# Filter inputs first, all sine tables at the beginning, weight conversions in two parts, and loads one step ahead, in a convolution and expert kernel

## The chip, the core and the metric

The kernel runs on one core of one Trainium2 chip. The metric is device time in microseconds (us), the median of several executions. Besides whole times, I quote the lengths of stages, read from one profiled execution of each kernel; the start of a stage is the start of its first matmul on TensorE.

## The reference

The first half is a long convolution by Fourier transforms, with a filter made by a two-layer network. The second half is an expert layer that multiplies its hidden values by their cosine.

```python
# x, v: (4, 12480, 128) float32; pos_emb: (12480, 64)
h_filt = (np.maximum(pos_emb @ w1, 0.0) @ w2) * np.exp(-0.01 * pos)[:, None]
u = x * v
Uf = np.fft.rfft(u, n=L, axis=1)            # L = 2 * 12480
Hf = np.fft.rfft(h_filt, n=L, axis=0)
y = np.fft.irfft(Uf * Hf[None], n=L, axis=1)[:, :12480, :]
z = (x * y).reshape(49920, 128)
h = z @ w_in                                # w_in (128, 2048), float64
out = (h * np.cos(h)) @ w_out               # w_out (2048, 128), float64
```

## The kernel before

A transform is two stages of matmuls, f1 and f2, with a twiddle between them; the inverse is i1 and i2. The sine tables are made on the chip. The float64 weights come as pairs of 32-bit words and are converted to float32 in eight pieces each. One batch is transformed at the start; the other three are interleaved with the expert matmuls through generators, whose yields say how many expert matmul steps pass before the next piece.

```python
def to_float32(pool, dst, raw):                      # one piece of a weight
    power = pool.tile([P, WCOL], U32, name="power")
    nc.vector.tensor_scalar(out=power, in0=hi, ...)           # exponent bits
    nc.gpsimd.tensor_scalar(out=power, in0=power, ...)        # twice
    nc.vector.tensor_scalar(out=sig, in0=hi, ...)
    nc.scalar.activation(high, sig, ...); nc.scalar.activation(low, lo, ...)
    nc.gpsimd.tensor_tensor(high, high, low, op=ALU.add)
    nc.vector.scalar_tensor_tensor(out=power, in0=hi, in1=power, ...)  # waits for GpSimd
    there = low if dst.space == DRAM else dst
    nc.gpsimd.tensor_tensor(there, high, power, op=ALU.mult)
    # ... store of there, if dst is in DRAM

# f1: one of two engines takes the whole eviction of matmul pair b
def f1_takers(b):
    if b % 2 == 0:
        return nc.scalar.copy, ...
    return nc.vector.tensor_copy, ...

def units(n, steps, before, mm, after, parts, ahead=2):
    for j in range(min(ahead, n)):
        before(j)                                    # loads
    # ... matmuls and evictions of n steps, with yields
    yield REST

REST = 1.5
U_STEPS, F1_STEPS, F2_STEPS, I1_STEPS, I2_STEPS = 2.0, 0.8, 3.3, 0.8, 1.5

def u_units(b, bufs, u, engine, side="left"):        # u = x * v, sums, differences
    # ... units(...) with u_multiply(tiles[j], half, engine), u_sums(...)
    clear_gap(u)                                     # a memset on GpSimd

# the start
for i in range(NCH):                                 # 11 chunks of filter rows
    if i + 3 < NCH:
        pes[i + 3] = filter_load(pool, i + 3)        # pe: 4 buffers
    if i + 1 < NCH:
        peTs[i + 1] = filter_turn(pool, bank, pes.pop(i + 1), ident)
    filter_hidden(pool, bank, aT, i, peTs.pop(i), w1_sb, windows[i])
    for _ in range(2):
        next(first_u)                                # x, v loads, products on GpSimd
    if i == 0:
        forward_tables(pool)                         # 6 sine tables on VectorE
# ... filter output beside u; f1 of the filter beside the rest of u
with tc.tile_pool(name="tables", bufs=1) as pool:    # in f1 of u
    inverse_tables(pool)                             # 10 sine tables on GpSimd
with tc.tile_pool(name="convert", bufs=1) as pool:   # w_in, beside the rest of f1
    convert = convert_units(pool, [(wind[:, c], w) for c, w in in_pieces])
    # ... one step of convert every 6 units
# ... f2; i1 beside the conversion of w_out; i2 and experts
```

## Time and profile before

The median was 3912.47 us (3909.58 to 3913.06, three runs). The stages below are used in the whole document.

| stage | what runs | from, us | length, us |
|---|---|---|---|
| A | filter layers, 11 chunks | 0 | 57.2 |
| B | filter output, beside u = x v | 57.2 | 36.9 |
| C | f1 of the filter, beside the rest of u | 94.1 | 47.0 |
| D | f1 of u, tables, w_in conversion | 141.1 | 87.7 |
| E | f2 of both | 228.8 | 105.2 |
| F | i1, w_out conversion | 334.0 | 70.2 |
| G | first i2 groups, to the first expert matmul | 404.2 | 24.0 |
| H | experts, with the other three batches between | 428.2 | 3481.5 |

In the profile, PE is TensorE, DVE VectorE, ACT ScalarE, POOL GpSimd and SP the queue that issues the transfers; PEld is TensorE loading its weights. An eviction is the copy of a finished matmul result out of PSUM, TensorE's result memory, by VectorE or ScalarE; until then its place there is not free: in D of the kernel before TensorE waited 18.5 us in all for such copies by ScalarE. ScalarE's instruction ACT_TABLE_LOAD stands twice in this trace, at 0.73 and at 13.08 us, 1.28 us each; these are the loads that the prediction counts. The granted clock is the share of TensorE's full clock that the profile records, 1.00 or 0.50 at any moment of the traces of the kernel before; in a longer window it is the mean. Behind a wait for the memset (L350), from 1512 to 1519 us, it was 0.52 in the kernel before, and 1.00 from 1519 to 1524 us. A line of the view of waits reads: engine, what it wanted to write, what it waited for, then us in total, times, longest. "L395" is line 395 of that kernel; the change moved the lines, so L374 before is L395 after. The prediction shows the lines of before that carry it.

### The profile page before, as it was taken

What the parts mean: (1) busy time and instruction counts of PE and PEld (TensorE: products, weight loads), DVE (VectorE), ACT (ScalarE), POOL (GpSimd) and SP (SyncE); (2) the same over time, 40 slices, a digit from 0 to 9 for tenths busy, and PEclk for the clock granted to TensorE, in tenths of its full rate; (3) what the DMA queues carried; (4) which work ended last, traced back from release to release, by engine and by line L of the source; (5) the groups of instructions that cost most, each with busy time, mean ns of one, the idle gap of its engine ahead of it and who ended that gap; (6) DMA issues with size and microseconds to landing.
All of it is one profiled execution on the core that took longest, in us unless ns stands there. A gap on an engine that the chain in (4) does not pass through costs nothing.

```text
span 3909.7 us, 47024 instructions
## 1 busy us (share of the span) xinstructions
PE 3740.2 (96%) x13450; PEld 2126.6 (54%) x13450; DVE 2783.3 (71%) x5739; ACT 2500.7 (64%) x4639; POOL 2596.0 (66%) x2340
## 2 busy tenths in 40 slices
PE   5798798999999999999999999999999999999999
PEld 3766554655456555654466555544466644444444
DVE  3787798677776787677776886777865566666666
ACT  3554566766665456766665556766655477777777
POOL 6555587468874565588854665588844477777776
PEclk7899899999999999999999999999999999999999
DMA  4143444012210562022201660122202500000000
GB/s 131 51 119 105 139 139 121 11 55 67 75 49 9 164 175 64 23 70 69 73 23 31 174 181 26 39 68 69 70 12 80 170 24 17 20 19 17 22 17 14
DMA packets 208363, 273.90 MB, mean 70 GB/s; under 512 B 16968, under 2 KB 145768, under 8 KB 207976
## 3 DMA queue, kind: packets, MB, share of 16 engines
q1 hardware_dynamic: 208104, 270.89, 24.0%
q8 instruction: 108, 1.77, 0.2%
q14 instruction: 151, 1.24, 0.1%
HBM read 191.57 MB, written 79.26 MB: 69 GB/s over the span
## 4 chain that ended last, share of the span: by engine, by line
PE 79%; POOL 4%; DVE 4%; ACT 3%; DMA 2%; issue 1%; SPq 0%; POOLq 0%; DVEq 0%; ACTq 0%
PE ph L651 31%; PE acc L676 26%; PE cv L676 5%; PE cv L447 4%; PE cv L422 4%; PE cv L374 3%; PE cv L404 3%; POOL f L660 3%; PE ph L123 2%; DMA hd<-h 1%; ACT cs L665 1%; DVE slots L432 1%; DVE k L657 1%; DVE xt L362 1%; DVE gt L667 1%
## 5 line engine op out<-in xcount | busy, mean ns | idle before, releaser
L660 POOL TENSOR_TENSOR f<-a,k 128x512 f32<-128x512 f32 x1568 | 1984.5, 1266 | 1060.7 <-DVE k L657 1051.4
L651 PE MATMUL ph<-at,w_in_sb 128*128 128x512 f32 x3136 | 1606.1, 593 | 17.3 <-DVE gt L667 16.9
L654 ACT ACTIVATE a<-ph,quarter 128x512 f32<-128x512 f32 x1568 | 1072.5, 684 | 802.5 <-PE ph L651 793.8
L676 PE MATMUL acc<-gt,w_out_sb 128*128 128x512 f32 x2688 | 1378.2, 594 | 8.2 <-ACT ot L682 8.1
L667 DVE TENSOR_TENSOR gt<-ph,cs 128x512 f32<-128x512 f32 x1568 | 1078.0, 687 | 319.8 <-ACT cs L665 294.0
L657 DVE TENSOR_SCALAR k<-a 128x512 f32<-128x512 f32 x1568 | 787.6, 502 | 636.2 <-ACT a L654 611.7
L665 ACT ACTIVATE cs<-f 128x512 f32<-128x512 f32 x1568 | 980.2, 625 | 343.9 <-POOL f L660 342.2
L676 PEld LDWEIGHTS acc<-gt,w_out_sb 128*128 128x128 f32 x2688 | 507.5, 190 | 663.7 <-issue 624.9
L651 PEld LDWEIGHTS ph<-at,w_in_sb 128*128 128x128 f32 x3136 | 556.2, 190 | 360.9 <-issue 262.4
L417 POOL TENSOR_TENSOR slots<-slots,t 120x256 f32<-120x256 f32 x384 | 312.1, 819 | 72.3 <-PE ps L404 37.0
L447 PEld LDWEIGHTS cv<-slots,tm 96*104 96x104 f32 x1920 | 245.4, 173 | 113.2 <-issue 100.4
L447 PE MATMUL cv<-slots,tm 96*104 96x128 f32 x1920 | 257.7, 278 | 16.8 <-DMA tm<-td 13.0
L676 PE MATMUL cv<-gt,w_out_sb 128*128 128x512 f32 (+1 forms) x448 | 222.2, 578 | 1.0 <-DVE gt L667 1.0
L422 PEld LDWEIGHTS cv<-cs,slots 120*96 120x96 f32 x1536 | 175.6, 167 | 65.3 <-issue 62.2
L422 PE MATMUL cv<-cs,slots 120*96 120x120 f32 x1536 | 182.2, 266 | 1.1 <-POOL slots L417 0.8
L374 PEld LDWEIGHTS cv<-c,slots 104*124 104x124 f32 x768 | 134.7, 195 | 85.8 <-issue 59.7
L404 PE MATMUL cv<-slots,w 124*120 124x256 f32 x576 | 173.0, 380 | 0.0
L374 PE MATMUL cv<-c,slots 104*124 104x192 f32 x768 | 153.8, 330 | 19.3 <-POOL slots L350 19.3
L404 PEld LDWEIGHTS cv<-slots,w 124*120 124x120 f32 x576 | 103.3, 184 | 121.9 <-issue 113.5
L368 POOL TENSOR_TENSOR slots<-xt 104x256 f32<-104x256 f32 x120 | 120.5, 1004 | 41.7 <-PE ph L651 19.1
L676 PEld LDWEIGHTS cv<-gt,w_out_sb 128*128 128x128 f32 x448 | 84.8, 190 | 102.5 <-issue 99.5
L432 DVE TENSOR_TENSOR slots<-cv,other 96x240 f32<-96x240 f32 x384 | 133.8, 395 | 5.4 <-ACT other L430 4.4
(121 smaller groups left out, 2564.6 us busy)
## 6 DMA issues: line engine op xcount, KB each, us to landing
h<-hd SPq DMA_DIRECT2D x144, 240.0 KB
tm<-td SPq DMA_DIRECT2D x90, 312.0 KB
xt<-in_x_dram SPq DMA_DIRECT2D x120, 208.0 KB
vt<-in_v_dram SPq DMA_DIRECT2D x120, 208.0 KB
xs<-in_x_dram SPq DMA_DIRECT2D x120, 208.0 KB
zd<-zs SPq DMA_DIRECT2D x120, 208.0 KB
zb<-zd SPq DMA_DIRECT2D x97, 256.0 KB
w<-wd SPq DMA_DIRECT2D x144, 116.2 KB
```

Source lines behind the costliest of these rows:

```text
L374: nc.tensor.matmul(ps[0:KE, i * 2 * N1:(i + 1) * 2 * N1], u[:, b, 0:KE, i], c1[0:u.shape[0], :, :].rearrange("p r k -> p (r k)"), start=Tr ...
L404: nc.tensor.matmul(ps[0:N2, i * 2 * D:(i + 1) * 2 * D], w[:, i, :], src[0:KE], start=True, stop=True)
L417: nc.gpsimd.tensor_tensor(y[:, r], y[:, r], t[:, r], op=op)
L422: nc.tensor.matmul(ps[0:N1, (i * 2 + r) * N2:(i * 2 + r + 1) * N2], parts[0:N2, r, :, b, i], cs[:, r, :], start=True, stop=True)
L447: nc.tensor.matmul(ps[0:R, i * D:(i + 1) * D], t[:, i, r, :], slots[0:N1, :, place, :], start=(r == 0), stop=(r == 1))
L651: nc.tensor.matmul(ph[:, 0:m], w_in_sb[:, c * P:(c + 1) * P], ats[n][:, 0:m], start=True, stop=True)
L654: nc.scalar.activation(a[:, 0:m], ph[:, 0:m], AF.Identity, bias=quarter[:, 0:1], scale=INV_TWO_PI)
L657: nc.vector.tensor_scalar(out=k[:, 0:m], in0=a[:, 0:m], scalar1=ROUND, scalar2=ROUND, op0=ALU.add, op1=ALU.subtract)
L660: nc.gpsimd.tensor_tensor(f[:, 0:m], a[:, 0:m], k[:, 0:m], op=ALU.subtract)
L665: nc.scalar.activation(cs[:, 0:m], f[:, 0:m], AF.Sin, scale=TWO_PI)
L667: nc.vector.tensor_tensor(gt[:, 0:m], ph[:, 0:m], cs[:, 0:m], op=ALU.mult)
L676: nc.tensor.matmul(accs[n][:, 0:m], w_out_sb[:, c, :], gt[:, 0:m], start=(c == 0), stop=(c == NFC - 1))
```

## The change

The intent is to give TensorE its filter inputs at once, to move table work out of D, to take VectorE's wait for GpSimd out of the conversions, and to have data ready when a later batch changes its stage. Cut to its core:

```diff
-def to_float32(pool, dst, raw):
-    power = pool.tile([P, WCOL], U32, name="power")
+def float32_parts(pool, raw):
+    power = pool.tile([P, WCOL], U32, name="power", bufs=2)
 ...                                   # as before, to the sum of high and low
+    return power, high
+def float32_join(dst, raw, power, high):
     nc.vector.scalar_tensor_tensor(out=power, in0=raw[:, :, 1], in1=power, ...)
-    there = low if dst.space == DRAM else dst
+    there = power.bitcast(F32) if dst.space == DRAM else dst
 ...                                   # convert_units: parts of piece i, then join of i - 1
+            if i < len(pieces):
+                half = float32_parts(pool, raws[i])
+            if i > 0:
+                float32_join(pieces[i - 1][0], raws[i - 1], *last)
 ...                                   # Tables: on VectorE; a yield before each Sin
+        yield
         nc.scalar.activation(dst, t, AF.Sin, scale=TWO_PI / turn)
 ...                                   # the inverse tables are stored to DRAM, reloaded before f2
 ...                                   # units(): a yield 0.0 behind the first loads
-REST = 1.5
-U_STEPS, F1_STEPS, F2_STEPS, ... = 2.0, 0.8, 3.3, ...
+REST = 3.0
+U_STEPS, F1_STEPS, F2_STEPS, ... = 2.0, 0.8, 2.9, ...
 ...                                   # u_units
+                if j == H // UA - 2:
+                    clear_gap(u)
-            clear_gap(u)              # behind the last sum
 ...                                   # i2 beside the next batch's u
-            if i >= 4:
+            if i >= 5:
 ...                                   # forward_units: first i2 loads ahead of i1
+    next(back)
     yield from i1_units(bank)
 ...                                   # the start: all pe first, then x and v
+                for i in range(1, NCH):
+                    pes[i] = filter_load(pool, i)
+                first_u = u_units(0, 3, slots,
+                                  lambda j, half: nc.gpsimd if half == 0 or 6 <= j < 18
+                                  else nc.vector)
                 for i in range(NCH):
-                    for _ in range(2):
-                        next(first_u)
+                    for _ in range(2):
+                        next(sines, None)
+                    if i >= 5:
+                        for _ in range(3):
+                            next(first_u)
 ...                                   # expert rows are loaded later in a block
-                if c == 0 and n + 2 < NALL:
+                if c == NFC - 4 and n + 2 < NALL:
                     load(n + 2)
```

## The prediction

> **What bounds the kernel now.** I began with the page, parts 1 and 2: busy time of each engine, then the span in 40 slices of 98 us.
>
> ```profile
> PE 3740.2 (96%) x13450; PEld 2126.6 (54%) x13450; DVE 2783.3 (71%) x5739; ACT 2500.7 (64%) x4639; POOL 2596.0 (66%) x2340
> PE   5798798999999999999999999999999999999999
> PEclk7899899999999999999999999999999999999999
> ```
>
> TensorE (PE) is busy 96% of the span; its unfilled slices are the first seven. So from some 690 us on only the gaps between matmuls can be won, and the rest must come from the start. I cut the span where the matmul line changes and asked for each stage's busy times (length, then PE, PEld, DVE, ACT, POOL, granted clock, DMA share, GB/s).
>
> ```profile
> 0.00:57.20 57.20, 23.61 (x67) 12.73 (x67) 10.63 (x38) 22.68 (x41) 28.66 (x45) 0.77 0.44 105
> 57.20:94.10 36.90, 28.47 (x120) 20.63 (x121) 26.49 (x75) 11.03 (x30) 34.76 (x46) 0.87 0.57 167
> 94.10:141.10 47.00, 45.70 (x256) 43.91 (x257) 42.66 (x172) 37.35 (x188) 26.45 (x43) 0.95 0.26 75
> 141.10:228.80 87.70, 61.58 (x258) 54.30 (x256) 52.67 (x152) 43.76 (x133) 46.87 (x71) 0.77 0.12 37
> 228.80:334.00 105.20, 96.44 (x384) 67.00 (x384) 92.33 (x287) 52.89 (x139) 67.82 (x96) 0.98 0.58 167
> 334.00:404.20 70.20, 56.32 (x512) 54.57 (x512) 47.69 (x155) 28.95 (x84) 32.12 (x34) 0.98 0.15 47
> 404.20:428.20 24.00, 13.43 (x76) 12.92 (x77) 9.54 (x23) 8.30 (x22) 8.15 (x11) 0.61 0.71 213
> 428.20:690.00 261.80, 232.22 (x859) 125.76 (x858) 232.50 (x385) 162.88 (x316) 204.27 (x178) 0.98 0.45 130
> 690.00:3909.70 3219.70, 3182.43 (x10925) 1734.79 (x10923) 2268.82 (x4456) 2132.91 (x3691) 2146.93 (x1819) 0.99 0.21 61
> ```
>
> In order: A, filter layers; B, filter output; C, the filter's first transform; D, that of u (with inverse sine tables and the w_in conversion); E, second transform; F, inverse transform with the w_out conversion; G, first groups of output, until the first expert matmul at 428.2; H, the last two rows, experts with the other batches between. In B POOL is the fullest (34.8 of 36.9). D is the hole: C has as many matmuls and takes 47 us, D 87.7, with no engine full. The chain of waits, on the stages D, F and H in turn (H: PE only), names what fills the holes.
>
> ```profile
> PE ps L374 <- ACT slots L381: 18.5, 5, 15.1
> DVE power L145 <- POOL power L134: 17.2, 8, 2.2
> DVE power L130 <- DMA raw<-in_moe_w_in_dram: 15.9, 1, 15.9
> ...
> DVE power L145 <- POOL power L134: 17.2, 8, 2.2
> ...
> PE cv L374 <- POOL slots L350: 19.3, 3, 6.5
> PE ph L651 <- DVE gt L667: 16.9, 15, 2.6
> PE cv L447 <- DMA tm<-td: 13.0, 3, 5.0
> ```
>
> DVE stands 15.9 us for the raw words of w_in, because their buffers lie where the table pool was and GpSimd finishes the tables only at 164; then 8 x 2.15 us for GpSimd in the middle of each conversion, with the evictions that free PE's PSUM banks queued behind. In H, three batches each pay a memset wait (L350) and a table load wait (tm).
>
> [...]
>
> ```profile
> 1515.36 1.64 PE L374 MATMUL cv<-c,slots 104*124 104x192 f32 x4 [6.52 <-POOL slots L350]
> 1516.79 1.91 PE L651 MATMUL ph<-at,w_in_sb 128*128 128x512 f32 x2
> 1518.50 1.30 PE L676 MATMUL acc<-gt,w_out_sb 128*128 128x512 f32 x2
> 1519.63 0.81 PE L374 MATMUL cv<-c,slots 104*124 104x192 f32 x4
> ```
>
> Start to start, the first four L374 take 1.43 us against 0.65 later, L651 1.71 against 0.86, L676 1.13 against 0.86: 1.9 us lost on top of the 6.5. [...] L145's wait holds ready evictions. [...] Here the 104x256 multiply takes 0.72 us on POOL, 0.41 alone on DVE. [...] The trace shows 1.28 us, and the instruction order of the changed kernel has two loads, as before, so interleaving sines with relus adds none.
>
> **The change part by part.**
>
> A. Before, SyncE's queue stood from 7.7 to 28.3 us at a vt load with no free buffer, pe loads behind it; PE waited 14.5 us for pe and 27.3 for ACT, itself behind six sines. Now all pe go first: 11 x 240 KB at the some 200 GB/s seen in the first slices is about 14 us. The chunks then run at PE's 2.4 us (its spacing at 32 to 37 us). Tables put on DVE 16 sines at about 1.05 us, some 17 us, beside that. From chunk 5 on POOL has 1.2 + 0.73 + 0.97 = 2.9 us a chunk: chunk 5 at about 27, the last done near 43. 44 instead of 57.2: **-13**.
>
> B. u now advances 38 units (12.7 pairs) here instead of 45 (15); POOL takes 2.43 us a pair, so 31 instead of 36.5, just over PE's 28.5. 32 instead of 36.9: **-5**.
>
> C. In exchange 11.3 pairs instead of 8 to 10 fall here, with half the multiplies on DVE: 11.3 x (0.43 + 0.45) = 10 us, against 5.6 us in the 42.7 now. DVE gets to 37 + 10 = 47 us plus waits for POOL and the vt load in its queue. Estimate 54: **+7**.
>
> D. Tables gone from here (10 sines on GpSimd), raw words loaded early. DVE's own work: 32 x (0.55 + 0.36 + 0.35), start to start 1.23 us = 39.4, and 8 conversions x 0.95 = 7.6: 47 us. The join is now queued 14 units (some 5 us) behind its parts, POOL needs 3.1 us for those, so no wait. PE needs 46, ACT 33 + 7. 49 with the start of E: **-39**.
>
> E. Same pools, same hd stores; DVE at 2.02 us for each of 48 steps sets it. **-1**.
>
> F. The joins' 17.2 us on DVE go; PE becomes the bound: 512 x 0.105 = 54, and a cold start. 56: **-14**.
>
> G. The four first x and v loads now come behind zb(0), which the first transpose waited 9 us for. 21: **-3**.
>
> Start: -13 - 5 + 7 - 39 - 1 - 14 - 3 = **-68**; the first expert matmul at about 360.
>
> H. clear_gap is issued two steps early: 19.3 us of waits and 3 x 1.9 of slow clock, 25. tm and xs are asked for before i1: 13.0 and about 9 of slow clock (2.6 to 3.3 each in the timeline), 22. The forced burst of 88 L422 at 1265 goes as well, by my count of the paces (some 358 expert steps to the next batch's output, the 31st group needed at 364 instead of 352), but it was work, not idling. Against this, 428 to 690 is close to DVE's limit (232.5 of 261.8), a pace of 3.4 instead of 3.5 gives DVE less time per group, and of each wait a little may stay: I give back 5. **-42**.
>
> Sum: -110 of 3912: about 3803.
>
> **Rivals.** *C takes it back.* DVE waits in turn for POOL and for vt in C, and PE's evictions stand behind, as the conversions' did in D. For: [...] x/v came at 170 GB/s in B. Against: vt waits were on POOL, and C has DMA at 0.26. If so +10 to +20: 3815 to 3823. *Nothing in H.* The wait for the memset may be a wait for the pipe: at 682.5 it ran directly behind the expert work (f, L660), and the last sum of u would then hold f1 as long. For: POOL ran sum, f, memset back to back. Against: three REST steps of 1.7 us now lie between that sum and f1, instead of half as many. If half stays, +12 to +20. *DVE full from 428 to 690.* It is 89% busy; faster pacing could open more gt waits (16.9 us): +5 to +10. *Better still:* A's first chunks or C cost less than said, -10.
>
> **Range and chances.** Start: A to C together some +-12, D +-8, F and G +-5; H +-12. In squares about 20 us, so 8 in 10 lie within some 26: 3778 to 3830. Faster by over 2% means below 3834: 0.91. Same 0.085, slower 0.005, since no part adds PE work.
>
> **What would show it.** First expert matmul near 360; first filter-output matmul near 44; f2 beginning near 180; no DVE wait of a join for POOL in D or F; PE waits for the memset and for tm together under 8 us after 428; PE idle there 35 us or so instead of 66. Wrong would be: DVE waits for xt in C over 10 us with C beyond 60 us; the memset's wait reappearing under the name of the sum; or E longer because the reloaded tables or w stores wait for freed memory.

## The result, and the profile after

The changed kernel took 3844.14 us in the median (3840.34 to 3847.06, four runs), beside 3912.19 us for the kernel before (3909.58 to 3913.06, four runs). The ratio is 0.9827, with a 95% interval of 0.981 to 0.9844. The time fell by 1.7%, about 68 us where 110 had been predicted, and so by less than the 2% to which the prediction had given 0.91.

The page of the changed kernel, busy times and two rows of the 40 slices:

```profile
PE 3728.1 (97%) x13450; PEld 2119.9 (55%) x13450; DVE 2819.6 (73%) x5803; ACT 2494.4 (65%) x4639; POOL 2551.1 (66%) x2274
...
PE   6988889999999999999999999999999999999999
...
PEclk8899999999999999999999999999999999999999
```

TensorE's count is the same and the start is still where it isn't full. The stages again (columns as in the prediction), here A, C, D, F and G:

```profile
0.00:52.20 52.20, 26.49 (x67) 12.98 (x67) 32.88 (x87) 23.32 (x51) 23.63 (x38) 0.74 0.43 110
...
84.20:149.65 65.45, 62.05 (x256) 56.07 (x257) 53.72 (x211) 37.46 (x189) 21.24 (x28) 0.72 0.30 87
149.65:207.70 58.05, 46.62 (x259) 44.74 (x257) 48.27 (x130) 40.83 (x122) 28.56 (x32) 0.92 0.15 42
...
313.10:372.30 59.20, 55.42 (x512) 54.94 (x512) 49.50 (x155) 28.48 (x85) 30.43 (x36) 0.96 0.18 55
372.30:396.00 23.70, 10.79 (x60) 10.44 (x61) 7.04 (x16) 6.46 (x17) 5.80 (x9) 0.66 0.52 156
```

C is longer than before although it has the same number of matmuls, at a granted clock of 0.72. Against the prediction:

| stage | before | predicted | after | after less predicted |
|---|---|---|---|---|
| A | 57.2 | 44 | 52.2 | +8 |
| B | 36.9 | 32 | 32.0 | 0 |
| C | 47.0 | 54 | 65.4 | +11 |
| D | 87.7 | 49 | 58.0 | +9 |
| E | 105.2 | 104 | 105.4 | +1 |
| F | 70.2 | 56 | 59.3 | +3 |
| G | 24.0 | 21 | 23.7 | +3 |
| first expert matmul at | 428.2 | 360 | 396.0 | +36 |
| H | 3481.5 | 3439.5 | 3442.6 | +3 |

H has the predicted length. The view of TensorE's waits after 396 us begins so; neither the memset nor tm is in it any more:

```profile
PE ph L677 <- DVE gt L693: 19.6, 18, 2.3
PE acc L702 <- ACT ot L708: 5.3, 11, 1.1
PE ph L126 <- DMA zb<-zd: 4.9, 2, 3.1
```

The start did not. Three views show what stood in its place.

**A.** The timeline of VectorE in the changed kernel (start, length, both in us), then of GpSimd and of ScalarE:

```profile
18.23 0.28 DVE L210 TENSOR_SCALAR moved<-prod,quarter_p 124x120 f32<-124x120 f32 x1
18.61 1.03 DVE L213 TENSOR_SCALAR turned<-moved 124x120 f32<-124x120 f32 x1
```

```profile
18.29 1.27 POOL L338 TENSOR_TENSOR slots<-relu,window 128x480 f32<-128x480 f32 x1 [3.09 <-ACT relu L336]
```

```profile
23.70 0.28 ACT L219 ACTIVATE tw_w<-turned 124x96 f32<-124x96 f32 x1 [1.92 <-DVE turned L217]
23.89 0.54 ACT L328 COPY peT<-ps 128x480 f32<-128x480 f32 x1
```

A table instruction that takes 0.19 to 0.28 us elsewhere took 1.03 us while GpSimd multiplied by the window. From 18 to 40 us this comes once in every chunk. L213 ends at 19.64 us, just behind GpSimd's end at 19.56. The last two lines show how that reaches TensorE: the Sin waits 1.92 us for VectorE, and the copy of the next chunk's input (peT), ready since its transpose on TensorE ended at 20.36 us, stands behind it until 23.89.

**C.** Slices of 5 us of the changed kernel, columns as above:

```profile
100.00:105.00 5.00, 5.00 (x32) 5.00 (x32) 4.71 (x18) 4.56 (x24) 2.22 (x3) 1.00 0.44 129
...
110.00:115.00 5.00, 3.72 (x20) 3.13 (x21) 4.71 (x17) 2.57 (x14) 3.07 (x4) 1.00 0.52 154
...
120.00:125.00 5.00, 4.98 (x16) 3.95 (x14) 4.74 (x20) 2.38 (x12) 1.46 (x2) 0.50 0.28 85
...
135.00:140.00 5.00, 4.99 (x15) 4.48 (x16) 2.79 (x12) 1.61 (x8) 0.00 (x0) 0.50 0.00 0
```

At first 32 matmuls pass in 5 us, then 20 with VectorE full (4.71 of 5), then 15 or 16 at half clock. At 135 us VectorE has room again (busy for 2.79 of 5), but TensorE is still at half clock, though it is recorded as busy for 4.99 of 5, as for 4.98 in the slice before. The view of TensorE's waits names ScalarE's evictions there (3.2 us in C) and not VectorE's; that VectorE sets the pace is read from its busy time, and tested below. The weight loads show what goes on from 132 us:

```profile
132.04 2.41 PEld L395 LDWEIGHTS ps<-c,ftile 96*124 96x124 f32 x8 [0.52 <-ACT slots L402]
134.97 2.41 PEld L395 LDWEIGHTS ps<-c,ftile 96*124 96x124 f32 x8 [0.52 <-ACT slots L402]
137.90 2.41 PEld L395 LDWEIGHTS ps<-c,ftile 96*124 96x124 f32 x8 [0.52 <-ACT slots L402]
140.84 6.25 PEld L395 LDWEIGHTS ps<-c,ftile 96*124 96x124 f32 x20 [0.52 <-ACT slots L402]
```

Matmuls start 0.32 us apart, but after every eight TensorE waits for an eviction, and that step takes 0.54 us. From 141 us this wait is gone, and at 147.74 us the clock is full again. This slow stretch lasted 30.7 us, from 117.02 us on. Three other executions with an unchanged C (see below) were read in windows of 20 us from 100 to 160 us; the slow time there comes to some 10 us in a0 (clock 1.00, 0.77, 0.97), some 17 us in y3 (1.00, 0.64, 0.94) and some 34 us in y5 (0.87, 0.50, 0.77). The 30.7 us are nine times 3.41 us; in the traces of the kernel before and of the changed one every slow stretch, but for the one that the trace's end cuts, is a whole multiple of 3.41 us. Cut into pieces of 3.41 us, the last piece of the 30.7 us held 11 matmul starts, and no earlier piece more than 10. So in this stretch the clock came back after the piece with the most starts. (A stretch of 6.8 us from 82.88 us ended after a piece of 10, so no rule is shown.)

**D.** The view of VectorE's waits in D of the changed kernel:

```profile
DVE power L133 <- DMA wind<-power: 5.8, 6, 1.8
DVE w L277 <- DMA wind<-power: 2.1, 1, 2.1
```

The wait for GpSimd is gone, and so is that for the raw words. A new one is there: a converted piece is now built in the tile power, which has two buffers, and the piece after next waits until it is stored.

### The profile page after: what moved, and what is told of

Same layout as the page of the kernel before. It is cut to its first block, busy times and chain, and to the rows that moved or that the text cites. A ratio compares the mean times of both kernels' runs of the same rounds, so it can differ in the third digit from the quotient of the medians.

```text
span 3838.6 us, 47111 instructions
## 1 busy us (share of the span) xinstructions
PE 3728.1 (97%) x13450; PEld 2119.9 (55%) x13450; DVE 2819.6 (73%) x5803; ACT 2494.4 (65%) x4639; POOL 2551.1 (66%) x2274
## 3 DMA queue, kind: packets, MB, share of 16 engines
q1 hardware_dynamic: 208822, 271.63, 24.2%
## 4 chain that ended last, share of the span: by engine, by line
PE 84%; DVE 5%; POOL 4%; ACT 3%; DMA 2%; issue 2%; SPq 0%; DVEq 0%; POOLq 0%; ACTq 0%
PE ph L677 32%; PE acc L702 27%; PE cv L702 5%; PE cv L468 5%; PE cv L443 4%; PE cv L395 3%; PE cv L425 3%; POOL f L686 2%; PE ph L126 2%; PE ps L395 1%; DMA hd<-h 1%; PE ps L443 1%; DVE k L683 1%; ACT cs L691 1%; DVE gt L693 1%
## 5 line engine op out<-in xcount | busy, mean ns | idle before, releaser
L702 PE MATMUL acc<-gt,w_out_sb 128*128 128x512 f32 x2656 | 1359.7, 593 | 5.6 <-ACT ot L708 5.3
L438 POOL TENSOR_TENSOR slots<-slots,t 120x256 f32<-120x256 f32 x384 | 310.7, 815 | 62.1 <-DVE t L437 23.8
L702 PE MATMUL cv<-gt,w_out_sb 128*128 128x512 f32 (+1 forms) x480 | 238.5, 579 | 1.0 <-DVE gt L693 1.0
L383 DVE TENSOR_TENSOR xt<-xt,vt 104x256 f32<-104x256 f32 x198 | 146.7, 743 | 1.2 <-DMA vt<-in_v_dram 0.9
```

The source lines that it names most:

```text
L438: nc.gpsimd.tensor_tensor(y[:, r], y[:, r], t[:, r], op=op)
L702: nc.tensor.matmul(accs[n][:, 0:m], w_out_sb[:, c, :], gt[:, 0:m], start=(c == 0), stop=(c == NFC - 1))
```

## The experiments

Each is one edit of the changed kernel, unless it says otherwise. Stage lengths in us, from the profiled execution of each:

| run | median us | ratio to before (95%) | A | B | C | D | F | G | first expert matmul | H |
|---|---|---|---|---|---|---|---|---|---|---|
| a0_after | 3843.49 | 0.9822 (0.9809–0.9836) | 52.2 | 32.1 | 59.8 | 57.9 | 58.6 | 23.5 | 389.8 | 3442.5 |
| x1_u_pool | 3837.39 | 0.9816 (0.9802–0.9829) | 52.2 | 32.7 | 49.7 | 64.0 | 59.6 | 24.1 | 390.5 | 3451.5 |
| x2_power3 | 3838.88 | 0.9813 (0.9800–0.9826) | 52.2 | 32.2 | 63.6 | 52.1 | 58.9 | 23.6 | 389.0 | 3447.6 |
| x4_win_dve | 3837.36 | 0.9816 (0.9802–0.9829) | 47.1 | 32.7 | 56.5 | 59.5 | 59.0 | 23.9 | 385.1 | 3443.1 |
| x3_zb | 3845.54 | 0.9834 (0.9819–0.9849) | 52.2 | 33.1 | 66.5 | 58.7 | 58.6 | 21.8 | 396.6 | 3451.8 |
| x5_act_evict | 3830.48 | 0.9791 (0.9777–0.9806) | 52.2 | 32.2 | 49.4 | 62.2 | 59.3 | 24.0 | 385.9 | 3442.5 |
| y1_no_back | 3838.38 | 0.9813 (0.9796–0.9829) | 52.2 | 32.2 | 59.8 | 58.9 | 59.6 | 24.2 | 393.2 | 3444.1 |
| y2_gap_late | 3858.99 | 0.9868 (0.9853–0.9882) | 52.2 | 33.1 | 66.5 | 58.0 | 59.0 | 23.7 | 398.1 | 3459.9 |
| y3_rest | 3860.56 | 0.9872 (0.9856–0.9889) | 52.2 | 32.5 | 61.5 | 58.4 | 59.6 | 23.6 | 393.8 | 3462.8 |
| y5_rest_no_back | 3878.06 | 0.9915 (0.9900–0.9930) | 52.2 | 32.6 | 66.5 | 58.9 | 58.7 | 23.8 | 398.1 | 3478.5 |
| y4_join_now | 3860.40 | 0.9869 (0.9854–0.9884) | 52.2 | 32.0 | 65.4 | 66.8 | 70.2 | 23.5 | 416.3 | 3442.6 |
| y6_pacing | 3848.40 | 0.9845 (0.9829–0.9862) | 52.2 | 33.2 | 61.5 | 59.1 | 59.4 | 24.3 | 395.3 | 3446.6 |
| z2_combo | 3815.36 | 0.9756 (0.9741–0.9770) | 47.3 | 32.9 | 47.6 | 53.1 | 58.8 | 23.6 | 369.4 | 3448.0 |
| s2_one_sine | 3837.78 | 0.9814 (0.9798–0.9831) | 38.0 | 41.3 | 60.0 | 57.7 | 58.4 | 23.6 | 386.0 | 3441.9 |
| z4_one_sine | 3815.07 | 0.9755 (0.9738–0.9771) | 38.5 | 41.3 | 46.4 | 53.2 | 58.4 | 23.9 | 367.4 | 3442.4 |

Two spreads must be known before anything is read from this. In ten executions where nothing up to the end of C was changed (the profiled one of the result, a0, x2, x3 and y1 to y6), C took 59.8 to 66.5 us; C and D together, leaving out x2 and y4, which change D, 117.7 to 125.4 with a mean of 121.9. And H, where nothing of H was changed, took 3441.9 to 3451.5 us. Most effects below are of that size in the whole time, so I judge them by stages.

### The base: a0_after

No edit.

> The changed kernel itself, as the base for the runs beside it. Both theories: 3840 to 3847 us, 1.7% under the kernel before; first expert matmul at 396 us, filter's f1 (C) 65 us, f1 of u with the w_in conversion (D) 58 us, filter layers (A) 52 us.

The time is as expected, C is 5.6 us shorter than in the execution of the result, at a granted clock of 0.87 against 0.72. The profiled execution was also the fastest of the four (3834.06 us, the others 3843.45 to 3844.43), so its short C is not typical; the spreads above serve better than this one base. So part of C's length is how long the slow clock happens to last. It is not all: in x4_win_dve below, C's clock was 0.95, and C still took 56.5 us with VectorE busy for 51.5. So VectorE's backlog does not bring the slow clock every time.

### C: x1_u_pool and x5_act_evict

```diff
-  lambda j, half: nc.gpsimd if half == 0 or 6 <= j < 18
+  lambda j, half: nc.gpsimd if half == 0 or 6 <= j
```

> Change: from pair 6 on every multiply of the first u is on GpSimd; none is on VectorE in C. Theory (VectorE falls behind in C, TensorE gets gaps, its clock drops to half and stays there): C goes from 65 to 50-54 us, the granted clock of C from about 0.7 to over 0.9, total -10 to -15 us. Rival (the 11 pairs cost C their transfers [...], whoever multiplies; the clock only follows): C stays above 61 us or the time comes back in B or D, total 0 to -4 us.

The stages C and D of this run:

```profile
84.88:134.61 49.73, 47.66 (x257) 44.03 (x257) 44.46 (x170) 37.48 (x189) 29.01 (x40) 0.94 0.39 115
134.61:198.64 64.03, 49.75 (x257) 46.30 (x257) 54.94 (x158) 40.83 (x122) 28.57 (x32) 0.91 0.13 38
```

C fell to 49.7 us, and the clock rose to 0.94, as the theory said. But D grew by 6 us, as the rival said: VectorE ran 158 instructions there instead of 130. TensorE had left C with evictions still queued on VectorE, and they came out of D. C and D together are 113.8 us, 8 below the mean of 121.9. The fall of the whole time, 6 us, isn't beyond the spread.

```diff
-def f1_takers(b):
-    if b % 2 == 0:
+def f1_takers(b, more=False):                  # more: in the two f1 stages of the start
+    if b % 2 == 0 or more and b % 16 == 7:
```

> Change: in the two f1 stages of the start (C and D) ScalarE takes 36 of 64 evictions in place of 32, VectorE 28. Theory (C and D together are bound by VectorE, busy 102 of 118 us in the base run, and TensorE's half clock in C follows from it): C + D goes from 117.7 to 106-111 us, total -7 to -12 us. Rival (TensorE's clock sets C and the stores set D; VectorE's share is incidental): C + D stays within 3 us of 117.7.

C and D together took 111.6 us, 10 below the mean and just short of what the theory expected. C's clock was 0.95 with VectorE's multiplies still in place, so it is VectorE's load and not those multiplies as such. One execution of x4 had that clock too, without this edit; but the clocks of whole executions agree: 0.987 to 0.991 in the four of x5, 0.983 to 0.985 in seven of eight of the changed kernel. D was longer here too, 62.2 us, with more waits for the store (10.3 us). The interval of the ratio lies below that of the base. The theory holds: **VectorE's work in C and D together** is most of what bounds them; x2 below takes 6 us off by store waits alone.

### D and F: x2_power3 and y4_join_now

```diff
-    power = pool.tile([P, WCOL], U32, name="power", bufs=2)
+    power = pool.tile([P, WCOL], U32, name="power", bufs=3)
```

> Change: three buffers of the tile power in place of two. Theory (in D a conversion waits for the store of the piece before last out of power): waits of VectorE for the store, some 16 us, go; D from 58 to 50-52 us, total -6 to -8 us. Rival (D is bound by VectorE's own 47 us and by the half clock with which it starts): waits move to another name, D stays over 55 us, total 0 to -3 us.

D took 52.1 us where an unchanged D took 57.7 to 59.5 in ten executions. The view of VectorE's waits in D has one store wait left, at the beginning of E:

```profile
DVE w L277 <- DMA wind<-power: 1.7, 1, 1.7
```

The theory holds for the stage, though it had put these waits at some 16 us and the base shows 7.5; the whole time fell by 4.6 us, within the spread. The rival's half clock at the start of D is not what the changed kernel shows: there the clock was full from 147.74 us, and D begins at 149.65.

```diff
             if i < len(pieces):
                 half = float32_parts(pool, raws[i])
-            if i > 0:
-                float32_join(pieces[i - 1][0], raws[i - 1], *last)
+                float32_join(pieces[i][0], raws[i], *half)
```

> One part undone: each conversion's join is queued directly behind its parts again, in both conversions; buffers as in the changed kernel. Theory (VectorE stands some 2.1 us per piece for GpSimd, with evictions behind it): D +10 to +17 us, F +5 to +12 us, total +15 to +28 us. Rival (the store waits and TensorE's work fill that time anyway): D and F together within 6 us of 116.5.

D rose to 66.8 us (+8.9 over the base, a little less than expected) and F to 70.2 (+11.6), which is F's length before the change; the whole time rose by 17 us. The old wait is back in D, and 17.2 us of it in F:

```profile
DVE power L151 <- POOL power L137: 17.4, 8, 2.3
```

So the split is all of F's gain and, in D, 9 us net: it removed 17.4 us and brought 8 us of store waits. The rest of D's gain of 30 is what else the change took away there, the tables and the late raw words, of which I made no separate experiment.

### A: x4_win_dve and s2_one_sine

```diff
-        nc.gpsimd.tensor_tensor(aT[:, 0:H, i * ROWS:(i + 1) * ROWS], t, window, op=ALU.mult)
+        nc.vector.tensor_tensor(aT[:, 0:H, i * ROWS:(i + 1) * ROWS], t, window, op=ALU.mult)
```

> Change: the filter layers' window multiply on VectorE in place of GpSimd. Theory (VectorE's table instructions, 0.21 us alone, take 1.0 to 1.2 us while GpSimd multiplies, and ScalarE's queue stands behind the sines that wait for them): table instructions go back to about 0.2 us, A from 52 to 44-47 us, total -5 to -8 us. Rival (ScalarE's own work of peT copy, relu and sines sets the pace of a chunk): A stays at 50-53 us, total within 2 us.

A fell to 47.1 us. Up to 35.6 us only one table instruction took more than 0.3 us, and that one lay beside a GpSimd multiply. The chunks still came every 3.14 us (relu to relu, mean from 16.34 to 35.20 us), against 3.29 before the edit (from 17.63 to 37.37 us); the larger part of the gain is in the last chunks, where GpSimd had both the window and u. So it was the multiply on GpSimd that had made these instructions long (1.03 us beside it, mostly under 0.3 us without it), but that was not all of it.

```diff
 # on top of x4_win_dve
-                    for _ in range(2):
-                        next(sines, None)
+                    next(sines, None)
```

> Change on top of the window multiply on VectorE: one sine table per chunk of the filter layers in place of two; the five left over follow the last chunk. Theory (two tables per chunk, about 2.1 us of VectorE beside the 0.66 us multiply, set the pace of 3.1 us): chunks come at 2.4 us, A goes from 47.1 to 42-44 us; the five tables left take VectorE 5 us in B, which GpSimd bounds, so B +0 to +3. Rival (the pace is ScalarE's own order or TensorE's): A stays at 46-47 us, and B grows by 3 to 5 us.

With one table per chunk, the first chunks came every 1.84 us (from 14.53 to 27.44 us) and A took 38.0 us. So the pace was set by **two tables per chunk on VectorE**, and not by TensorE: the 2.4 us of the prediction was no floor. The edit takes a sine off ScalarE as well, but in x4 ScalarE was busy for only 8.3 of the 18.9 us from 16.34 to 35.20 us, VectorE for 15.8. But B grew by 8.6 us, well over what either theory had expected, and A and B together stayed at 79.4 (79.8 in x4). The waits of B name the reason:

```profile
POOL ftile L371 <- DMA twd<-tw_t: 8.0, 1, 8.0
```

The tile ftile, which B fills, is opened where the pool of the tables was closed. The last tables now end behind the last chunk, and their store holds that memory. The first wait of this kind was known (raw behind the tables, in the kernel before, 15.9 us); I had not looked for the next.

### G: x3_zb

```diff
-            if i >= 5:
+            if i >= 7:
```

> Change: the next batch's x and v loads start two steps later in the output loop, so that the load of the first expert rows (zb) comes ahead of the first two xt and vt loads in the queue. Theory (zb stands 12.9 us behind them, this is what G's expected 3 us went to): PE's wait for zb goes from 12.9 to about 9 us, G from 23.5 to 20-21 us, total -3 us. Rival (zb waits for its own producer, the store of the second output group): G stays at 23-24 us.

The load of zb came ahead of x and v in the queue, TensorE's wait for it fell from 12.9 (11.2 in a0) to 9.6 us, and G from 23.5 to 21.8. Even so, it was issued 4.2 us after the issue of the second store of zd (389.31 against 385.10 us), 5.8 us in the changed kernel. The rest of the wait is thus that for its own producer, as the rival had it. H was 3451.8, just above the spread, and the whole time no better: no gain shown.

### H: y1_no_back, y2_gap_late, y3_rest, y5_rest_no_back, y6_pacing

```diff
 # y1_no_back
-        next(back)
```

> One part undone: the first tm and xs loads of the next batch's output are no longer asked for before its inverse transform i1. Theory (as predicted: this part took 13.0 us of tm waits and about 9 us of slow clock out of H): +15 to +22 us, and PE waits for tm near 13 us come back after 428 us. Rival (H's gain came from the pacing and the earlier memset; the load would be hidden anyway now): within 4 us.

The rival was right: H was 3444.1, tm was waited for 1.3 us in all. This part, to which the prediction gave 22 us, has no effect that shows while the pause is 3.0.

```diff
 # y2_gap_late
-                if j == H // UA - 2:
-                    clear_gap(u)
 ...
+            clear_gap(u)
```

> One part undone: the memset of the gap is again issued after the last sum of u. Theory (as predicted: 19.3 us of waits and 3 x 1.9 us of slow clock hung on its place): +15 to +25 us, PE waits for the memset near 19 us come back. Rival (the longer pause before f1, REST 3.0 in place of 1.5, hides it now): within 4 us.

H was 17.4 us longer than in the base, and TensorE's wait for the memset is back: 11.2 us in three times, where it was 19.3 in the kernel before. The theory holds in time, not in the size of the wait: something else had already taken 8 us of it.

```diff
 # y3_rest; y5_rest_no_back has this and the edit of y1_no_back
-    REST = 3.0
+    REST = 1.5
```

> One part undone: the pause at each stage's end is 1.5 expert steps again in place of 3.0. Theory A (the early memset and the early tm load take the waits away by themselves): H stays within 5 us of 3442.5, no wait of PE for tm, memset or sum over 1 us. Theory B (the longer pause hides them; the early memset only helps): 6 to 20 us more in H, with PE waits of 2 to 4 us at each of the three changes from u to f1.

Theory B. H was 3462.8, 20.3 us more. In the view of TensorE's waits two lines are new, at f1 and at i1 of the later batches:

```profile
PE cv L395 <- DVE gt L693: 8.9, 3, 3.6
PE cv L443 <- POOL slots L438: 6.0, 6, 1.9
```

The memset has become early, so f1 now waits for something else at the same place. The view names the releaser that came last, an expert product on VectorE, but f1 does not read gt. In the timeline GpSimd's last sum of u (L389), which f1 does read, ends at 655.00 us and f1 begins at 655.05; at the other two places it is the same within 0.06 us. So f1 most likely waits for that sum. The longer pause fills the time with expert matmuls.

> Two parts undone: pause of 1.5 steps and no early tm and xs load. Undoing the early load alone cost nothing, so either the pause or the end of the forced burst had already taken the tm wait away. If the pause did: PE waits for tm of 2 to 5 us at each of three batches come back, 8 to 22 us more than with the pause alone undone. If the burst did (the load came late only where i1 ran at full speed): at most 4 us more.

H was 3478.5, another 15.7 us, and nearly the 3481.5 of the kernel before. The waits of y3_rest stay, and these come on top:

```profile
PE cv L468 <- DMA tm<-td: 6.0, 1, 6.0
...
PE cv L468 <- issue: 5.1, 1, 5.1
```

So the pause and the early load each remove the tm wait alone. With the pause, the load has nothing left to do; without it, it is worth 16 us.

```diff
 # y6_pacing
-    ... F2_STEPS ... = ... 2.9 ...;  FIRST_STEPS, I2U_STEPS = 3.4, 3.0
+    ... F2_STEPS ... = ... 3.3 ...;  FIRST_STEPS, I2U_STEPS = 3.5, 3.1
 ...                                   # and the loads of rows at c == 0, as before
```

> One part undone: the paces are those of before (F2 3.3, first 3.5, later 3.1; the pause stays 3.0), and the loads of expert rows are issued at the start of a block as before, so the forced burst before 1270 us comes back. Theory (the burst was work and not idling, as predicted): H within 5 us of 3442.5. Rival (the burst holds experts back and TensorE waits for evictions meanwhile): H +8 to +20 us, with PE waits for evictions of i1.

H was 3446.6, within 5 us as the theory said and inside the spread of unchanged H. No effect is shown; if there is one, it is about 4 us. The later loads of rows have a price, though: the wait for zb in H of the changed kernel (4.9 us, shown above) is absent from y6 and from the kernel before.

### Together: z2_combo and z4_one_sine

The edits of x1, x2, x4 and x5 in one kernel.

> Four changes together: window multiply on VectorE, all later u multiplies on GpSimd, three power buffers, 36 of 64 evictions of the two start f1 stages on ScalarE. Theory (A by the shared multiply, C and D by VectorE and the store waits): A 47, C 47-50, D 50-53 us, first expert matmul at 370-376 us in place of 390, total -16 to -24 us, near 3822 us. Rival (the gains overlap, as each shortens the same VectorE queue): first expert matmul at 380-385 us, total -8 to -12.

The first expert matmul was at 369.4 us and the time 3815.36, which beats both kernels: 2.4% less than before. Most of the gains added up: C and D took 100.7 us, 21 below the mean, where x1 (8), x5 (10) and x2 (6) had shown 24, and x4's execution, at 116.0, another 6. In whole time, z2 is 28 us below a0, and the falls of the four single runs sum to 30. D, at 53.1, did not grow as it had in x1 and x5.

> The same on top of the four changes together. Theory: first expert matmul at 365-368 us in place of 369.4, total 1 to 5 us under 3815. Rival: 369 to 373 us, total the same or above.

367.4 us to the first expert matmul and 3815.07 in all. The medians of z2 and z4 are the same; A's 9 us go to B as in s2_one_sine.

## Why the prediction was right or wrong

The predicted time was too low by 41 us, and the range missed. Direction, B, E, F's mechanism and, by luck, the size of H were right; nearly all the miss lies in A, C and D.

- **A, wrong.** The failing step is "The chunks then run at PE's 2.4 us (its spacing at 32 to 37 us)", with the tables' 17 us put "beside that". They were not beside it: on ScalarE each chunk's copy stood behind a Sin (23.89 behind 23.70 us above), and that Sin waited for VectorE (1.92 us). Two tables make 2.1 us of a chunk, and the one instruction beside GpSimd's multiply adds 0.8 to 1.0 (1.01 to 1.16 us in place of 0.19 to 0.28). Measured 3.29 us per chunk, 3.14 with that multiply on VectorE, 1.84 with one table. With one table A was shorter than the expected 44 us, but B paid for it. Two readings behind this step were wrong as well: the 2.4 us was a single spacing at a granted clock of 0.50, so not TensorE's own pace; and "27.3 for ACT" looks like one wait counted twice (13.1 on PE, 14.3 on PEld).
- **B, right**: 32.0 us.
- **C, wrong, term mis-sized, then a consequence not seen.** The step is "DVE gets to 37 + 10 = 47 us". The 37 us came from a window of the kernel before that held only 27 to 28 of the 32 evictions of VectorE; the other five had run into D. All 32 are about 43 us (32 x 37/27.5), so 53, and 53.7 to 54.6 were measured. This equals the estimate for the whole stage, with no room for a single wait. VectorE fell behind, TensorE got gaps, and in all six executions with an unchanged C whose clock was read the clock fell to half for a time (mean 0.72 in C of the changed kernel, 0.73 in y4, 0.76 in x2; 0.77 in a0, 0.64 in y3 and 0.50 in y5 from 120 to 140 us). With less on VectorE, in x1 and x5, C had no such stretch (0.94 and 0.95); in x4 (0.95) it stayed away without that. The rival "C takes it back" (+10 to +20) had the right stage and size, but its mechanism, VectorE's own waits for GpSimd and vt, came to 4.6 and 0.5 us in B and C together.
- **D, wrong, a wait took the place of the one removed.** "The join is now queued 14 units (some 5 us) behind its parts [...] so no wait" was right, there is no join wait. But the sum had no term for the piece's store, which now holds power: 8 us of VectorE's waits. With a third buffer D is 52.1, 3 from the predicted 49.
- **F, right in mechanism**: the joins are the gain, by y4. The start at half clock (to 318.4 us, the first 5.3 us of F) and the rest were 3 us more than "54, and a cold start. 56".
- **G, wrong**: "The four first x and v loads now come behind zb(0)" did not happen. In the changed kernel the loads of xt and vt were issued from 382.9 to 385.2 us, zb at 388.0. The extra yield at a stage's start moved the count by one, so that i >= 5 falls where i >= 4 fell. And where it does happen, x3 shows 1.7 us.
- **H, right in size, wrong in its parts.** -38.9 against -42. But the step "tm and xs are asked for before i1: 13.0 and about 9 of slow clock" is not what did it: y1 puts it at 1.6 us. The earlier memset, given 25, is worth 17.4 (y2). The pause, which the prediction only used as an argument against a rival, is worth 20. That rival ("the last sum of u would hold f1 as long") is most likely what y3 shows when the pause is short. The right total of H came of parts that compensate, so it was luck.

With the four causes taken away, the first expert matmul comes at 369.4 us against a predicted 360. Of the 9 us left, A is 3, F 3, G 3 and E 2, while C and D are 2 better than predicted. These are not settled further. Nor is it settled what starts the slow clock of C in a given execution: a0 had some 20 us of gaps in TensorE's work before it came, and x4 had them without it. What was measured at its end is under C above.

## What to carry to other kernels

When work moves between stages, count what each window really held (instructions, not busy time), and add up the fullest engine over the stages on both sides: a shorter stage can hand its queue to the next. For each buffer that gets a new role, ask who reads it last, and how long that takes; the wait for a store (8 us in D) or for closed memory (8.0 us in B of s2_one_sine) is as real as the one removed. And undo the parts of a change one by one and in pairs before crediting one of them: a pause and an early load removed the same wait here, each alone.
